# A recurrent attention block and a mixture of experts on one core: turning x later in six units, a small transfer's user later in one, a warm-up in shorter matmuls

## The chip, the core and the metric

The kernel runs on one core of one Trainium2 chip. The core has a matrix engine (PE, with its weight loads PEld), a vector engine (DVE), a scalar engine (ACT), a programmable engine (POOL) and SP, which here only issues transfers. Each engine works through its own list of instructions in order; semaphores tie them together. The metric is the device time of one execution in microseconds, inputs and outputs in the chip's memory, as the median of repeated runs.

## What is computed

```python
# q, k, v, f_logit: (4, 8, 768, 48);  f = sigmoid(f_logit)
for t in range(S):
    state = f[:, :, t, :, None] * state + einsum('bhd,bhe->bhde', k_t, v_t)
    y[:, :, t] = einsum('bhd,bhde->bhe', q_t, state)
x = y.transpose(0, 2, 1, 3).reshape(3072, 384)
g   = argmax(x @ w_group)                 # 4 groups
e   = argmax(x @ w_expert[g])             # 4 experts in the group
out = g_weight * e_weight * (relu(x @ w1[g, e]) @ w2[g, e])    # 384 -> 1024 -> 384
```

All numbers are 32-bit. g_weight and e_weight are the softmax values of the chosen group and expert.

## The kernel before

The kernel has two halves. The first turns the recurrence into matmuls over chunks of 128 time steps and routes the tokens as it goes; the second runs the experts.

**Units.** The sequence has 6 chunks (NC) and 4 batch entries, taken two at a time: 12 units (NU), unit i being chunk i // 2 and half i % 2. For each unit there is a set of stages, written as Python generators. Each token in an order string, such as `t` or `x-1`, runs one further piece of one stage: the letter names the stage, the number is added to the unit of the turn (`x-1` in turn 5 works on unit 4). The stages that matter here:

- `l` (L584): SP issues the loads of k, q, v and of the next f.
- `c` (L593), `g` (L600): clamp f on DVE; then on ACT Exp and Ln, on PE the running sum `cs` (L616), on ACT the two exponentials eq and kh (L617, L618) of each of two batch entries; the last row of eq is sent to the small tile `ends` (L623), from POOL for units below 10 and from ACT for units 10 and 11 (`side`, L573).
- `m` (L630): q and k times these factors, on DVE.
- `t` (L642): four groups of turnings tr_q, tr_k on PE and their copies to Tq and Tk on ACT.
- `b` (L654): in odd units, `ends` is turned on PE (gt, L659) and copied on ACT to `decays` (L660).
- `z` (L663): two ACT copies that shift half of v.
- `s` (L670): scores ap on PE, masked on DVE to am (L692 in units 3 to 8, L707 in the others).
- `n` (L710): first piece, 32 matmuls ds on PE; second piece, state = (state + ds) * decays on DVE (L727, L728).
- `w` (L733): first piece, y from the state (L742); second piece, y from am and v (L754 or L746), copied on ACT to xT (L757).
- `d` (L760): logits lT from xT (L770), ACT copy lgT (L772); then lg (L775) and a DVE sum (L776). After an odd unit this starts the routing of the chunk.
- `x` (L782): *turning of outputs to rows*. Eight turnings x_ps on PE in two groups (L795), three ACT copies to rows in on-chip memory (L797, L800), and as a third piece, from unit 8 (KEPT) on, a transfer of the rows to x_dram (L803). Rows of units 0 to 7 are kept and sent by SP in turns 8 and 9 (`o`, L810).
- `r`: the next piece of routing (`route`, L188): A and B, maxima and one-hot choices on DVE; C, the ranks rk in five bf16 matmuls (L213, L215) and an Exp on ACT (L216); D, the places (pick, keys, run, L221 to L224) on DVE, and in turn 9 also the choice of the first experts (`rank_early`, `named`: who, L300); E and F, tables on DVE; G, the weight of each token (L246 to L254) and its transfer; H, a table tb on PE.
- `1` to `4` (`load_next`, L817): weights of the first two experts, by `who`.

**What sets the order.** Under `manual_schedule` the four engines PE, DVE, ACT and SP run their instructions in the order in which the Python code issues them, so an order string is the order on all four queues at once. POOL's order and the waits come from the framework. Turns 3 to 12 use EVEN, ODD or an entry of ORDERS (L847 to L855). BEGIN (L843) covers units 0 to 2.

**Buffers.** All outputs of PE but one share 7 banks (tag "bank", L81); a new tile takes a bank whose tile is done with.

**The second half.** 16 experts are sorted by load; one takes pass after pass of up to 230 tokens through two layers (hp L450, yo L486 or L471), gathered by POOL from x_dram and scattered by POOL to the output.

**Warm-up.** Before the first data are there, PE runs ten matmuls of ones into one bank (L891 to L893).

Of the kernel before, what the change touches and what calls it, by code (L numbers as in the profile page):

```python
# [18 lines left out]
P = 128  # L19
# [4 lines left out]
def kernel(  # L24
# [12 lines left out]
    nc = tc.nc  # L37
# [39 lines left out]
    def const(shape, dtype, name):  # L77
        return cp.tile(shape, dtype, tag=name, name=name)

    def bank(shape, name):  # L80
        return ps.tile(shape, FP32, tag="bank", name=name)  # L81
# [11 lines left out]
    onesb = const([P, P], BF16, "onesb")  # L93
# [305 lines left out]
    def fetch(pool, rows, n, top=N, late=False):  # L399

        w = {"n": n, "pool": pool, "early": top < N, "late": late, "blocks": [(j, min(P, n - j * P)) for j in range((n + P - 1) // P)]}
        w["x"] = pool.tile([P, len(w["blocks"]), RW], FP32, tag="xg", bufs=2 if pool is ep else 6, name="xg")
        for j, m in w["blocks"]:
            nc.gpsimd.indirect_dma_start(out=w["x"][:, j, :], out_offset=None, in_=x_dram[0:1 + top, :], in_offset=bass.IndirectOffsetOnAxis(ap=rows[:, j:j + 1], axis=0))  # L404
        return w
# [124 lines left out]
    with ExitStack() as fast:  # L530
# [31 lines left out]
        NU = len(units)  # L562
# [21 lines left out]
        def load(i, names):  # L584
            c, s = units[i]
            w = live.setdefault(i, {"v": pads["v"][i % 4], "qh": pads["qh"][i % 3]})
            for nm in names:
                if nm not in w:
                    w[nm] = sb.tile([P, 2, H, D], FP32, tag="ld_" + nm, bufs=3 if nm == "f" else 2, name="ld_" + nm)
                for b in parts(i) if nm == "f" else (slice(0, 2),):  # L590
                    nc.sync.dma_start(out=heads(w[nm][:, b])[:, :, 0:D], in_=SRC[nm][2 * s + b.start:2 * s + b.stop, :, c * P:(c + 1) * P, :].rearrange("b h t d -> t (b h) d"))
# [241 lines left out]
        def advance(gens):  # L833
# [10 lines left out]
            t1 t1 t1 t1 b1 c2 g2 g2 s1 s1 s1 s1 p d0 g2 g2 n0 n1 w1 w1 m2 m2 l4 n1  # L844
            d0 x1 x1 t2 t2 t2 t2 c3 g3 g3 x1 s2 s2 s2 s2 w2 g3 g3 d1 w2 n2 m3 m3 c4 g4 g4""".split()
        BEGUN = 3
        EVEN = "l+2 d-2 n-1 r r r x-1 x-1 t t t t g+1 g+1 x-1 r z s s w s s c+2 d-1 g+2 w g+2 n m+1 m+1".split()  # L847
        ODD = "l+2 d-2 r r x-1 x-1 t t t t b n-1 g+1 g+1 x-1 r z s s w s s c+2 d-1 g+2 w g+2 n m+1 m+1 r n".split()
        ORDERS = {
            NU - 4: "l+2 o d-2 n-1 r r r x-1 x-1 t t t t g+1 g+1 x-1 r z s s w s s c+2 d-1 g+2 w g+2 n m+1 m+1".split(),  # L850
            NU - 3: "l+2 o d-2 r r x-1 x-1 t t t t b n-1 r g+1 g+1 x-1 r s s s s c+2 w d-1 g+2 w g+2 n m+1 m+1 r n".split(),
            NU - 2: "d-2 r x-1 x-1 r t t t t g+1 g+1 r 1 x-1 s s s s w d-1 w n m+1 m+1 2 3".split(),
            NU - 1: "d-2 r r n-1 x-1 x-1 t t t t r x-1 r s s s s 4 w b d-1 w r r".split(),
            NU: "d-2 r e d-1 x-1 x-1 d-1 x-1 r r r e e r e r r e r r e r e r r e e e e e".split(),
# [3 lines left out]
        def step(nm, i):  # L858
            if nm == "r":
                advance(routes)  # L860
            elif nm == "e":
                next(first[0], None)
            elif nm == "p":
                next(pad)
            elif nm == "o":
                send_kept(i - (NU - 4))
            elif nm in "1234":
                load_next(*((0, 1), (1, 1), (0, 2), (1, 2))[int(nm) - 1])
            elif nm == "h":
                next(turning)  # L870
            elif 0 <= i < NU:
                if nm == "l":

                    load(i, ("k", "qh"))
                    if i + 1 < NU:
                        load(i + 1, ("f",))
                    load(i, ("v",))
                    return
                if (nm, i) not in steps_of:
                    steps_of[nm, i] = STAGES[nm](i)  # L880
                next(steps_of[nm, i], None)
# [6 lines left out]
        load(1, ("qh", "k"))  # L888
        load(2, ("f",))
        load(1, ("v",))  # L890
        warm = bank([P, 4, P], "warm")  # L891
        for _ in range(10):
            nc.tensor.matmul(warm, lhsT=onesb, rhs=onesb.unsqueeze(1).broadcast_to((P, 4, P)), start=True, stop=True)  # L893
        for tok in BEGIN:
            step(tok[0], int(tok[1:] or 0))
        for i in range(BEGUN, NU + 1):
            if i == BEGUN:
                nc.sync.dma_start(out=x_dram[0:1, 0:DM].rearrange("o (h d) -> o h d", d=D), in_=blank[:, 0:D].unsqueeze(1).broadcast_to((1, H, D)))
                nc.sync.dma_start(out=x_dram[0:1, DM:RW], in_=blank[:, D:D + 2])
            for tok in ORDERS.get(i, ODD if i % 2 else EVEN):  # L900
                step(tok[0], i + int(tok[1:] or 0))
# [62 lines left out]
    for n in range(GE - 1):  # L964
        w = ws[n]
# [105 lines left out]
    with tc.If(more > 0), ExitStack() as late:  # L1071
# [5 lines left out]
        with tc.For_i(0, last, 1) as i:  # L1077
# [14 lines left out]
            w = fetch(ep, row, P, late=True)  # L1092
# [32 lines left out]
```

## Time and profile before

| what | value |
|---|---|
| median of 3 runs | 418.54 us (418.44 to 419.1) |
| the profiled execution: its time | 417.84 us |
| the profiled execution: span, first to last instruction | 416.0 us |
| mean granted PE clock | 0.994 |
| PE busy / DVE busy / ACT busy, 40 to 60 us | 19.45 / 15.31 / 16.38 of 20 us |
| the same, 100 to 120 us | 18.98 / 17.23 / 12.26 of 20 us |
| the same, 160 to 180 us | 17.41 / 10.61 / 3.16 of 20 us |
| first half ends (last lg of the logits) | about 132 us |
| x_ps: turnings, median ns of one | 96, 273 (starts 109 ns apart) |
| ACT copies of x: 384 wide / 192 wide | 478 / 332 to 339 ns |
| longest DVE wait for `decays` (4 in all) | 6.0 us in total, 1.72 in unit 9 |
| warm-up: 10 matmuls, ns min/median/max | 379 / 631 / 631, first at 1.05, last at 4.7 us |

How to read it: the span is shorter than the time because the time holds what lies around the instructions. A matmul's duration includes its way through the array; neighbours overlap, so the distance between two starts tells the pace. "Busy" of PE counts overlapping ends as one. A line in order of time has the start, the duration (or the union of several), the engine, the line of the kernel, the operation with output and inputs, and, in brackets, how long the engine had been idle before it and what ended that. "ACTq" or "SPq" is the engine's sequencer, at work on something like the issue of a transfer.

### The profile page before, as it was taken

The numbers are of one execution on the slowest core, as the hardware profiler recorded it, in microseconds if no ns is written. First come the engines' busy times: TensorE is split into PE (matmuls) and PEld (weight loads), VectorE is DVE, ScalarE is ACT, GpSimd is POOL, SyncE is SP. The second block draws the span as 40 slices with busy tenths as digits, with TensorE's granted clock in tenths as the row PEclk, the third lists the DMA queues.
The fourth block names the chain that finished last, engine by engine and source line by source line (L and its number), as shares of the span: only waits on it lengthen the run. The fifth ranks groups of instructions, "written<-read, shape, count | busy, mean of one in ns | idle before, by whom it ended". The sixth has DMA issues, their size and how long they took to land.

```text
span 416.0 us, 10268 instructions
## 1 busy us (share of the span) xinstructions
PE 404.0 (97%) x4143; PEld 371.9 (89%) x4143; DVE 264.3 (64%) x783; ACT 162.2 (39%) x365; POOL 85.7 (21%) x132
## 2 busy tenths in 40 slices
PE   8999999999999997999999999999999999999994
PEld 3888888888888966989999999999999999999992
DVE  6666878787998702440799767485595595584230
ACT  6777878887664211211223122222231232232220
POOL 5000010101040174001041221311321230120230
PEclk9999999999999999999999999999999999999999
DMA  9999987879869499855729467586495596485010
GB/s 191 208 216 197 201 179 147 164 159 289 244 225 378 163 337 345 318 179 184 271 84 335 137 245 265 164 315 208 170 348 169 217 352 200 173 318 162 28 48 24
DMA packets 132146, 88.99 MB, mean 214 GB/s; under 512 B 102582, under 2 KB 122748, under 8 KB 132090
## 3 DMA queue, kind: packets, MB, share of 16 engines
q1 hardware_dynamic: 125666, 75.50, 60.6%
q0 software_dynamic: 5792, 11.92, 9.5%
q10 hardware_dynamic: 632, 0.83, 0.6%
q8 instruction: 35, 0.57, 0.6%
q14 instruction: 21, 0.17, 0.1%
HBM read 78.71 MB, written 9.83 MB: 213 GB/s over the span
## 4 chain that ended last, share of the span: by engine, by line
PE 48%; issue 30%; DMA 9%; POOL 6%; DVE 3%; POOLq 1%; another core or an unknown queue 1%; ACT 1%; SPq 0%; ACTq 0%; DVEq 0%
PE hp L450 12%; PE yo L486 6%; DMA out_dram<-yt,xg 6%; PE yo L471 4%; PE cs L616 4%; POOL out_dram L461 4%; PE ap L704 3%; PE y L746 3%; POOL xg L404 2%; PE x_ps L795 2%; PE tr_q L650 2%; PE tr_k L650 2%; PE y L742 2%; PE ap L689 2%; PE y L754 2%
## 5 line engine op out<-in xcount | busy, mean ns | idle before, releaser
L450 PE MATMUL hp<-xe,w 128*128 128x128 f32 (+14 forms) x864 | 141.3, 323 | 2.6 <-issue 1.8
L450 PEld LDWEIGHTS hp<-xe,w 128*128 128x128 f32 x864 | 137.4, 192 | 4.5 <-issue 2.4
L486 PE MATMUL yo<-h,w 128*128 128x230 f32 (+13 forms) x672 | 115.8, 333 | 0.0
L433 DVE STREAM_TRANSPOSE yr<-yT 32x192 f32<-32x192 f32 (+1 forms) x208 | 70.5, 339 | 70.5 <-ACT yT L487 67.9
L486 PEld LDWEIGHTS yo<-h,w 128*128 128x128 f32 x672 | 113.7, 190 | 0.2
L451 ACT ACTIVATE h<-hp 128x256 f32<-128x256 f32 (+14 forms) x72 | 34.2, 478 | 109.1 <-PE hp L450 100.2
L426 DVE STREAM_TRANSPOSE xe<-xg 32x192 f32<-32x192 f32 (+1 forms) x208 | 69.6, 335 | 8.7 <-PE hp L450 5.8
L461 POOL DMA_INDIRECT out_dram<-yt,xg x32 | 34.5, 1078 | 156.1 <-ACT yt L458 150.5
L487 ACT COPY yT<-yo 128x230 f32<-128x230 f32 (+13 forms) x42 | 13.5, 325 | 80.5 <-PE yo L486 80.5
L404 POOL DMA_INDIRECT xg<-x_dram,rows_p x30 | 29.6, 986 | 51.1 <-DMA out_dram<-yt,xg 25.7
L471 PE MATMUL yo<-w,h 128*128 128x384 f32 x64 | 21.3, 486 | 0.0
L707 DVE TENSOR_TENSOR am<-ap,tri 128x512 f32<-128x512 f32 x24 | 15.1, 688 | 7.3 <-PE ap L704 7.3
L616 PE MATMUL cs<-ld_f,tri 128*128 128x384 f32 x48 | 18.5, 505 | 0.5 <-POOL blank L177 0.3
L471 PEld LDWEIGHTS yo<-w,h 128*128 128x128 f32 x64 | 11.9, 190 | 7.4
L458 ACT ACTIVATE yt<-yr,xg 128x384 f32<-128x384 f32 (+13 forms) x26 | 14.4, 604 | 5.4 <-DVE yr L433 5.4
L623 POOL DMA_DIRECT2D ends<-eq x10 | 5.4, 542 | 52.2 <-ACT eq L617 52.2
L692 DVE TENSOR_TENSOR am<-ap,seen 128x384 f32<-128x384 f32 x24 | 12.2, 551 | 5.5 <-PE ap L689 5.5
L757 ACT COPY xT<-y 128x512 f32<-128x512 f32 x24 | 13.4, 587 | 5.0 <-PE y L746 4.4
L651 ACT COPY Tk<-tr_k 128x512 f32<-128x512 f32 x24 | 15.2, 636 | 0.0
L651 ACT COPY Tq<-tr_q 128x512 f32<-128x512 f32 x24 | 15.0, 625 | 0.4 <-PE tr_q L650 0.3
L441 DVE COPY xe<-xg_ps 128x384 f32<-128x384 f32 (+1 forms) x4 | 2.1, 535 | 20.5 <-remote 9.7
L650 PE MATMUL tr_q<-ident,qh 128*128 128x128 f32 x96 | 14.5, 274 | 0.5 <-issue 0.5
(187 smaller groups left out, 448.4 us busy)
## 6 DMA issues: line engine op xcount, KB each, us to landing
w<-in_moe_w_dram SPq DMA_DIRECT2D x34, 1536.0 KB, 7.2
qh<-in_q_dram SPq DMA_DIRECT2D x12, 384.0 KB, 6.1
ld_k<-in_k_dram SPq DMA_DIRECT2D x12, 384.0 KB, 4.4
v<-in_v_dram SPq DMA_DIRECT2D x12, 384.0 KB, 5.4
ld_f<-in_f_logit_dram SPq DMA_DIRECT2D x11, 384.0 KB, 5.5
x_dram<-x_kept SPq DMA_DIRECT2D x2, 1536.0 KB
x_dram<-x POOLq DMA_DIRECT2D x2, 384.0 KB
x_dram<-x ACTq DMA_DIRECT2D x2, 384.0 KB, 7.4
```

The source lines that it names most:

```text
L404: nc.gpsimd.indirect_dma_start(out=w["x"][:, j, :], out_offset=None, in_=x_dram[0:1 + top, :], in_offset=bass.IndirectOffsetOnAxis(ap=rows ...
L426: squares(w, lambda n, k_, rk, g, rg: nc.vector.transpose(out=xT[rg, 0:n, k_], in_=x[rk, 0:n, g]))
L433: squares(w, lambda n, k_, rk, g, rg: nc.vector.transpose(out=y[rk, 0:n, g], in_=yT[rg, 0:n, k_]))
L450: nc.tensor.matmul(hp[:, o, :], lhsT=w1[:, ko, (f + o) * P:(f + o + 1) * P], rhs=w["xT"][:, ko, :], start=(ko == 0), stop=(ko == KO - 1))
L451: nc.scalar.activation(h[:, f:f + 2, :], hp, AF.Relu)
L461: sent = nc.gpsimd.indirect_dma_start(out=out, out_offset=bass.IndirectOffsetOnAxis(ap=w["x"][0:m, j, DM + 1:RW].bitcast(U32), axis=0), in ...
L471: nc.tensor.matmul(yp, lhsT=w["h"][:, fo, :], rhs=w2[:, fo, :], start=(fo == 0), stop=(fo == FO - 1))
L486: nc.tensor.matmul(yp, lhsT=w2[:, fo, m * P:(m + 1) * P], rhs=w["h"][:, fo, :], start=(fo == 0), stop=(fo == FO - 1))
L616: nc.tensor.matmul(cs.rearrange("t h d -> t (h d)"), lhsT=tri, rhs=nl[:, b], start=True, stop=True)
L650: nc.tensor.transpose(out=pt[:, a, :], in_=w[nm + "h"][:, b, 2 * a:2 * a + 2, :].rearrange("t r d -> t (r d)"), identity=ident)
L651: nc.scalar.copy(w["T" + nm][:, b], pt)
L707: nc.vector.tensor_tensor(am[:, r], ap[r], tri.unsqueeze(1).broadcast_to((P, HP, P)), OP.mult)
```

## The change

Three things are edited. In turns 3 to 8 the three pieces of `x-1` go from ahead of (two) and behind (one) `t` and `g+1` to behind the masked scores and `d-1`, ahead of `w`'s second piece; `d-1` goes ahead of `c+2`; in ODD one `r` (piece C of the routing) goes behind `x-1` too. In turn 9, `b n-1` goes from ahead of `r g+1 g+1` to behind it. The warm-up becomes 40 matmuls of 128 columns in place of 10 of 512.

```diff
-        EVEN = "l+2 d-2 n-1 r r r x-1 x-1 t t t t g+1 g+1 x-1 r z s s w s s c+2 d-1 g+2 w g+2 n m+1 m+1".split()
-        ODD = "l+2 d-2 r r x-1 x-1 t t t t b n-1 g+1 g+1 x-1 r z s s w s s c+2 d-1 g+2 w g+2 n m+1 m+1 r n".split()
+        EVEN = "l+2 d-2 n-1 r r r t t t t g+1 g+1 r z s s w s s d-1 x-1 x-1 x-1 c+2 g+2 w g+2 n m+1 m+1".split()
+        ODD = "l+2 d-2 r r t t t t b n-1 g+1 g+1 z s s w s s d-1 x-1 x-1 x-1 r c+2 g+2 w g+2 n m+1 m+1 r n".split()
         ORDERS = {
-            NU - 4: "l+2 o d-2 n-1 r r r x-1 x-1 t t t t g+1 g+1 x-1 r z s s w s s c+2 d-1 g+2 w g+2 n m+1 m+1".split(),
-            NU - 3: "l+2 o d-2 r r x-1 x-1 t t t t b n-1 r g+1 g+1 x-1 r s s s s c+2 w d-1 g+2 w g+2 n m+1 m+1 r n".split(),
+            NU - 4: "l+2 o d-2 n-1 r r r t t t t g+1 g+1 r z s s w s s d-1 x-1 x-1 x-1 c+2 g+2 w g+2 n m+1 m+1".split(),
+            NU - 3: "l+2 o d-2 r r x-1 x-1 t t t t r g+1 g+1 b n-1 x-1 r s s s s c+2 w d-1 g+2 w g+2 n m+1 m+1 r n".split(),
...
-        warm = bank([P, 4, P], "warm")
-        for _ in range(10):
-            nc.tensor.matmul(warm, lhsT=onesb, rhs=onesb.unsqueeze(1).broadcast_to((P, 4, P)), start=True, stop=True)
+        warm = bank([P, P], "warm")
+        for _ in range(40):
+            nc.tensor.matmul(warm, lhsT=onesb, rhs=onesb, start=True, stop=True)
```

## The prediction, made before the changed kernel was run

> **What bounds the kernel now.** I read the page first, then a table of stretches, then the tensor engine, the scalar engine and the vector engine in order of time around unit 9, where the one visible hole lies. The page's first line says that the whole kernel is the tensor engine's:
>
> ```profile
> PE 404.0 (97%) x4143; PEld 371.9 (89%) x4143; DVE 264.3 (64%) x783; ACT 162.2 (39%) x365; POOL 85.7 (21%) x132
> ```
>
> By stretches (PE busy, then weight loads, DVE, ACT, POOL, granted clock, DMA share, GB/s), units 3 to 8 run from about 37 to 99 us:
>
> ```profile
> 40.00:60.00 20.00, 19.45 (x478) 16.65 (x477) 15.31 (x43) 16.38 (x38) 2.04 (x4) 1.00 0.91 182
> 60.00:80.00 20.00, 19.99 (x484) 17.26 (x482) 15.87 (x45) 16.53 (x38) 2.01 (x4) 1.00 0.76 153
> 80.00:100.00 20.00, 19.99 (x484) 17.26 (x483) 15.87 (x45) 16.52 (x38) 2.01 (x4) 1.00 0.97 218
> 100.00:120.00 20.00, 18.98 (x304) 16.00 (x304) 17.23 (x54) 12.26 (x31) 2.44 (x4) 1.00 0.78 207
> ```
>
> PE has no hole worth a name in the six units whose order changes: 0.53 us with no releaser at 56.5 (in unit 4), nothing after. A busy PE need not be a PE at its pace, so I also looked at starts: eight turnings x_ps start every 109 ns, in every unit; y L754 takes 1.64 us from first to last start in units 3, 5, 6, 7 and 8 alike, although DVE reaches its masks at different times in even and odd units. So PE is paced by its own work there. The 1.0 us missing from the last row is in unit 9. PE in order of time (start, us, what, idle before it and what ended it):
>
> ```profile
> 101.41 0.60 PE L650 MATMUL tr_k<-ident,kh 128*128 128x128 f32 x4
> 103.03 0.20 PE L659 MATMUL gt<-ident,ends 16*128 16x16 f32 x1 [1.02 <-DMA ends<-eq]
> ...
> 103.31 0.57 PE L616 MATMUL cs<-ld_f,tri 128*128 128x384 f32 x1
> ```
>
> PE stands before gt until the small transfer of `ends` lands (the chain of waits has it issued at 95.89 and on its way 7.01 us). Last to next start is 1.30 us. What follows on ACT, then on DVE:
>
> ```profile
> 102.23 0.67 ACT L651 COPY Tk<-tr_k 128x512 f32<-128x512 f32 x1
> 103.27 0.17 ACT L660 COPY decays<-gt 128x16 f32<-128x16 f32 x1 [0.38 <-PE gt L659]
> 103.34 0.27 ACT L216 ACTIVATE dl<-dl 128x80 f32<-128x80 f32 x1
> 104.24 0.49 ACT L617 ACTIVATE eq<-cs 128x384 f32<-128x384 f32 x1 [0.63 <-PE cs L616]
> 104.63 0.48 ACT L618 ACTIVATE kh<-cs 128x384 f32<-128x384 f32 x1
> 105.00 0.50 ACT L617 ACTIVATE eq<-cs 128x384 f32<-128x384 f32 x1
> 105.37 0.51 ACT L618 ACTIVATE kh<-cs 128x384 f32<-128x384 f32 x1
> 105.53 0.76 ACTq L623 DMA_DIRECT2D ends<-eq  x1
> ```
>
> ```profile
> 101.21 0.55 DVE L727 TENSOR_TENSOR st<-st,ds 128x384 f32<-128x384 f32 x1
> 103.47 0.56 DVE L728 TENSOR_TENSOR st<-st,decays 128x384 f32<-128x384 f32 x1 [1.72 <-ACT decays L660]
> 103.95 0.22 DVE L221 TENSOR_TENSOR pick<-rk,run 128x64 f32<-128x64 f32 x1
> ...
> 106.78 0.16 DVE L300 CAST who<-names 1x2 int32<-1x2 f32 x1
> 106.85 2.46 DVE L707 TENSOR_TENSOR am<-ap,tri 128x512 f32<-128x512 f32 x4
> ```
>
> From 103.47 to 109.3 DVE has no idle time. Its four masks am begin the moment `who` is done, and PE takes them at once (lT, then y L746, which needs am):
>
> ```profile
> 107.80 0.64 PE L770 MATMUL lT<-xT,gw 128*32 128x128 f32 x16
> 108.37 0.44 PE L746 MATMUL y<-am,v 128*64 128x128 f32 x4
> ```
>
> The first two am end near 108.07, the fourth at 109.31; y's second half starts near 109.4. So in unit 9 PE and DVE are level to 0.3 us and then to 0.1 us: whatever moves L728 moves PE.
>
> **What the Trainium skill says.** (1) Perfetto Trace Analysis, Sequencer Loop: a sequencer reads in order; an engine instruction is pushed into the engine's queue, a control instruction is executed by the sequencer before it reads on. The trace agrees for DMA issues: SP's start at 68.86, 69.32 and 70.56, each when the one before it (0.37, 1.15 us) is over. A copy behind L623 on ACT should thus wait out its 0.76 us. (2) TensorE: Matmul & The Clock Gate, "Why this matters for your kernels": PE should have no idle gaps over about 3 us, or its clock falls to half. The trace agrees: PE was mostly idle from 159.6 to 164.3, and the granted clock is 0.50 in 166 to 168. (3) The same page, Back-to-back issue gap: cold, matmuls start N/1.2 ns apart. The ten warm-up matmuls (N = 512) started some 0.43 us apart: agrees.
>
> **The change, part by part.**
>
> *x-1 in units 3 to 8.* The same eight turnings and three ACT copies, later. Removed: lg to x_ps 0.16 us, 0.87 us of x_ps, 0.11 to tr_q; lT to y 0.20. Added: lg to tr_q 0.16, lT to x_ps 0.20 (so at 130.9), x_ps to y 0.1 to 0.2. Sum per unit 0 to +0.09, six units 0 to +0.5. I take 0. Cover for what loses its distance: tr_q would start where x_ps did, 68.88 in unit 6; qh was ready at 67.96, kh at 68.83 against tr_k at 69.32, and both come some 0.87 us sooner, since the second ap, and behind it am, ld_f, qh and kh, come sooner in the unit. ACT's copies of x (1.1 us) fall into its waits before lgT (0.89) and before L607 (0.66); then L607 ends at about the time y is done, so xT is not late. If that cover is gone, xT is late by tenths. Banks: between y and its copy five others must serve am, lT, x and rk; the two of the second ap are free when the masks are done, before rk. SP: x_kept of unit 7 is ready near 97, and SP sends it at 106.13: covered. POOL's `ends` and meta come up to 0.87 us sooner in unit 8.
>
> *The r moved in units 3, 5, 7.* Five matmuls of rk (0.12 us) and one Exp (0.3 us), no DVE work; its user, pick, comes after kh. Nothing.
>
> *b and n-1 in unit 9.* Gain on PE: behind tr_k now come rk (0.12) and cs (1.4), so `ends` has landed when gt comes near 103.4. 1.30 less 0.1 of handover: 1.2 us. Loss: decays, a copy on ACT, now stands behind dl, eq, kh, eq, kh *and* the issue of unit 10's `ends`. Step by step: tr_k ends near 101.85, rk, cs from 102.0; the old eq began 0.93 after cs, so eq at 102.97 (ACT is also busy till then: Tk at 102.23 takes a slot of 0.48, dl 0.26); kh 103.36, eq 103.73, kh 104.10. The issue waits for eq (0.53 after its start, as before): 104.26 to 105.02. decays 105.05 to 105.3. L728 at 105.3 instead of 103.47: **+1.8 us**. Behind it on DVE, in order: pick to `who` (2.9 us), am, ld_f, qh, kh. PE could have y L746 at 107.2, but the first two am end near 109.87 and the fourth at 111.1: y's second half starts at 111.2, not 109.4. So PE saves 1.2 us, waits 2.7, and leaves unit 9 1.8 us late. Lower bound of this term: if the issue holds up nothing, decays runs at 104.5 and L728 at 104.8, +1.3.
>
> *After that.* Units 10 to 12 are dense on PE (holes of 0.26 and less), so nothing is won back; `who_late` for the early weights, who at 143.71 and all loads behind them hang on the same DVE chain and shift with it, as does the stretch 158 to 164, whose releaser the trace can't name. +1.8 goes to the end.
>
> *Warm-up.* 40 x 128 columns instead of 10 x 512: the same 5,120. Own weight loads: 40 instead of 10, 147 ns each, beside matmuls. Before, it ended at 5.06 and cs began at 5.35. If loads are hidden (107 ns a matmul by that same page): the same end. If not (254 ns until the clock rises at 4.5): end near 8, 1.6 us lost on the chain that runs through cs at 6.42. From below: 0, since cs waits for its data. I take 0. Sixty more PE instructions also shift where PE's instructions are fetched; the 0.53 us in unit 4 may go or come twice: -0.5 to +0.5.
>
> *Sum.* Against the profiled execution (span 416.0, time 417.84): span 417.8, time 419.6. The three runs have the median 418.54, so 418.54 + 1.8 = **420.3**.
>
> **Rivals.**
> - *Clock falls too.* PE's 2.7 us of idle in unit 9 is near the gap of point 2. Half speed for 3.4 us costs up to 1.7 us: 421.9. For it: a stretch in which PE worked about a third of the time did it at 164. Against: that one lasted 4.7 us.
> - *The other side: the hole before gt is all that counts, 417.2.* It needs L728 not to be late: decays would have to run by 103.5, which nothing on ACT's list allows unless L728's follower on DVE isn't what y waits for. PE's 1.2 us would then reach the end. It decides once am's start is set by ap (near 105.7) and not by `who`. A vanished 0.53 us in unit 4 would add to it. I also count here a shorter stall at 158 to 164.
> - *Given back: 418.6.* The delay is 1.3, and 0.5 in unit 4 and some of the later stall offset it.
>
> **How the numbers follow.** Forecast 0.45, clock 0.22, given back 0.10, faster 0.23. The forecast's own range is 419.5 to 421.1 (+1.3 from below, +0.5 of turnings and +0.3 of fetch from above). For 8 in 10 the clock case comes in whole and about half of the faster one: 417.4 to 422.2. A measurement of this kernel tells about 0.2%, 0.84 us, from no change: slower by more 0.65, within 0.12, faster by more 0.23.
>
> **What would show it.** In unit 9: no DMA wait before gt; DVE idle of about 3.5 us before L728, ended by ACT's decays, which starts right after the ACT issue of `ends`; PE idle of 2 to 3 us before y L746, ended by DVE. Units 3 to 8: 10.0 to 10.3 us each, as before, x_ps between lT and y, no new wait above 0.1 us. Wrong if decays starts before 104, if y L746 follows lT at once, or if PE is idle before tr_q, tr_k or rk in units 3 to 8.

## The result, and the profile after

| | before | after |
|---|---|---|
| median | 418.48 us (417.19 to 419.45, 9 runs) | 420.55 us (419.35 to 421.89, 9 runs) |
| the profiled execution: time / span | 417.84 / 416.0 | 421.04 / 419.2 |
| mean granted clock in it | 0.994 | 0.989 |

The changed kernel takes 1.0048 times as long, with an interval of 1.0029 to 1.0068: 2.0 us more, between 1.2 and 2.8. The two profiled executions stand 3.2 apart, since that of before is 0.64 below its median and that of after 0.49 above.

The page of the changed kernel, its line of busy times and its line of the granted clock in tenths over 40 slices:

```profile
PE 406.1 (97%) x4173; PEld 375.7 (90%) x4173; DVE 264.8 (63%) x783; ACT 162.8 (39%) x365; POOL 85.3 (20%) x132
PEclk9999999999899999899999999999999999999998
```

The busy times hardly differ. The clock line shows two dips, in the eleventh slice (105 to 115 us) and in the seventeenth; the second belongs to the stall near 160 us that the kernel before has too, the first is new.

**Where the time went.** I followed one landmark per unit, the first matmul ds (L722), through both traces. Before, those of units 2 and 8 start at 36.77 and 98.20, that of unit 9 at 110.30; after, at 37.18, 98.67 and 113.09. So the changed kernel is 0.41 late ahead of turn 3 already, loses 0.06 over the six units with the turning moved, and 2.32 in unit 9 (2.54 up to the next lg, since its ds start while the last of y is still running). Then nothing comes back: lg of units 10 and 11 is 2.97 late both times, the span 3.2.

Unit 9 of after, first ACT and then DVE (start, duration, what, idle before it and what ended that):

```profile
103.17 0.35 ACT L216 ACTIVATE dl<-dl 128x80 f32<-128x80 f32 x1
103.38 0.53 ACT L617 ACTIVATE eq<-cs 128x384 f32<-128x384 f32 x1
...
104.51 0.55 ACT L618 ACTIVATE kh<-cs 128x384 f32<-128x384 f32 x1
104.70 0.76 ACTq L623 DMA_DIRECT2D ends<-eq  x1
105.50 0.17 ACT L660 COPY decays<-gt 128x16 f32<-128x16 f32 x1 [0.45 <-ACT kh L618]
```

```profile
101.68 0.55 DVE L727 TENSOR_TENSOR st<-st,ds 128x384 f32<-128x384 f32 x1
105.71 0.56 DVE L728 TENSOR_TENSOR st<-st,decays 128x384 f32<-128x384 f32 x1 [3.48 <-ACT decays L660]
106.19 0.22 DVE L221 TENSOR_TENSOR pick<-rk,run 128x64 f32<-128x64 f32 x1
...
109.00 0.16 DVE L300 CAST who<-names 1x2 int32<-1x2 f32 x1
109.08 2.46 DVE L707 TENSOR_TENSOR am<-ap,tri 128x512 f32<-128x512 f32 x4
```

The copy of decays now stands behind six things on ACT (dl, two pairs of eq and kh, and an issue), and its bracket hides the last of them: what it waited for by the profile is kh, over at 105.06, but between the two stands the issue of a transfer, 104.70 to 105.46. L728 waits 3.48 for it (1.72 before). Everything that follows on DVE, down to `who` and the masks am, is as dense as before and starts later. PE, which has nothing to wait for at gt any more:

```profile
103.92 0.23 PE L659 MATMUL gt<-ident,ends 16*128 16x16 f32 x1
104.08 2.06 PE L704 MATMUL ap<-Tq,Tk 48*128 48x128 f32 x32
106.06 1.10 PE L742 MATMUL y<-Tq,st 48*64 48x128 f32 x32
107.09 0.65 PE L770 MATMUL lT<-xT,gw 128*32 128x128 f32 x16
109.81 3.55 PE L746 MATMUL y<-am,v 128*64 128x128 f32 x31 [2.07 <-DVE am L707]
```

The hole ahead of gt is gone, and a hole of 2.07 ahead of y L746 is there instead. And the matmuls of y then take 3.55. The same matmuls take 1.97 where the masks are ready (e4 below) and 2.9 where the masks come as late as here but the clock is full (e6 below); here they run at half the clock. In windows of 3.41 us (PE busy, weight loads, DVE, ACT, POOL, granted clock, DMA share, GB/s):

```profile
102.46:105.88 3.42, 3.42 (x43) 2.58 (x39) 0.17 (x1) 2.77 (x8) 0.00 (x0) 1.00 1.05 246
105.88:109.29 3.41, 1.86 (x54) 1.30 (x50) 3.07 (x14) 0.27 (x1) 0.00 (x0) 1.00 0.83 188
109.29:112.71 3.42, 2.90 (x24) 2.60 (x26) 3.42 (x6) 0.66 (x1) 0.00 (x0) 0.50 1.03 371
```

After a window in which PE was busy 1.86 of 3.41 comes one at 0.50.

### The profile page after: what moved, and what is told of

It reads as the page before. It is cut to its first block, busy times and chain, and to the rows that moved or that the text cites. A ratio compares the mean times of both kernels' runs of the same rounds, so it can differ in the third digit from the quotient of the medians.

```text
span 419.2 us, 10334 instructions
## 1 busy us (share of the span) xinstructions
PE 406.1 (97%) x4173; PEld 375.7 (90%) x4173; DVE 264.8 (63%) x783; ACT 162.8 (39%) x365; POOL 85.3 (20%) x132
## 3 DMA queue, kind: packets, MB, share of 16 engines
HBM read 78.71 MB, written 9.83 MB: 211 GB/s over the span
## 4 chain that ended last, share of the span: by engine, by line
PE 50%; issue 29%; DMA 7%; POOL 6%; DVE 4%; POOLq 1%; another core or an unknown queue 1%; ACT 1%; ACTq 0%
PE hp L450 12%; DMA out_dram<-yt,xg 7%; PE yo L486 6%; PE yo L471 4%; POOL out_dram L461 4%; PE cs L616 3%; PE y L746 3%; PE x_ps L795 3%; PE y L754 2%; PE ap L704 2%; PE ap L689 2%; POOL xg L404 2%; PE ds L722 2%; PE y L742 2%; PE tr_k L650 2%
## 5 line engine op out<-in xcount | busy, mean ns | idle before, releaser
L746 PE MATMUL y<-am,v 128*64 128x128 f32 x192 | 13.5, 293 | 2.1 <-DVE am L707 2.1
L746 PEld LDWEIGHTS y<-am,v 128*64 128x64 f32 x192 | 11.7, 148 | 3.8 <-DVE am L707 3.2
```

The lines of the kernel that those rows point to most:

```text
L746: nc.tensor.matmul(ys[b][DP * h:DP * h + DP, a, :], lhsT=w["v"][:, b, 2 * a + (b ^ h), :], rhs=w["am"][b][:, b ^ h, a, :], start=(c == 0 a ...
```

## The experiments

They ran on three other chips, four kernels on each, beside the kernel before. There the kernel before takes 412.43 (e1 to e4), 412.19 (e5 to e8) and 411.96 (e9 to e12); the stall near 160 and its half clock are absent in the traces of these runs. Ratios are to the kernel before on the same chip. My theory was that turn 9 makes the loss, by ACT's order (decays behind an issue) and DVE's order (all that PE needs behind L728); the rivals were the turning in six units, the warm-up, and the clock.

**e1: the turning alone** (turns 3 to 8 as in the change, the rest as before; of the three order strings edited, EVEN is shown).

```diff
-        EVEN = "l+2 d-2 n-1 r r r x-1 x-1 t t t t g+1 g+1 x-1 r z s s w s s c+2 d-1 g+2 w ...
+        EVEN = "l+2 d-2 n-1 r r r t t t t g+1 g+1 r z s s w s s d-1 x-1 x-1 x-1 c+2 g+2 w ...
```

> The kernel before with the turning moved in turns 3 to 8 alone. Theory (the loss sits in unit 9): 418.5 plus 0 to 0.3: in the changed kernel the even units 6 and 8 took 10.29 us from ds to ds instead of 10.05, with PE waiting for val before tb; three such waits cost 0.7, the 0.6 us stall of unit 4 may or may not be there, and the ends transfer, issued up to 0.5 us sooner, takes as much off the wait before gt. Rival (the move of the turning is what costs): at least +1.5, 420 or more.

Measured: 412.47 (14 runs), ratio 1.0006, 0.9996 to 1.0016. No change that can be told. But the trace has a longer wait, three times, in the even units. Waits from 36 to 99 us (in total, times, longest), first of e5, which is the kernel before, then of e1:

```profile
PEld L261 <- DVE val L243: 1.9, 3, 0.6
```

```profile
PEld L261 <- DVE val L243: 2.6, 3, 0.9
PE tb L261 <- DVE val L243: 0.8, 3, 0.3
```

tb, the matmuls of piece H, now comes 0.87 earlier after `t`, and `val` on DVE doesn't. The weight loads waited before too, at no cost, since PE was still busy; what is new is that PE itself waits. In starts of PE it costs 0.22 to 0.24 in each of units 4, 6 and 8 (10.29 from ds to ds, where an undisturbed even unit of the old order takes 10.07). What pays for it is e5's matter.

**e2: turn 9 alone.**

```diff
-            NU - 3: "l+2 o d-2 r r x-1 x-1 t t t t b n-1 r g+1 g+1 x-1 r s s s s c+2 w d-1 g+2 w g+2 n m+1 m+1 r n".split(),
+            NU - 3: "l+2 o d-2 r r x-1 x-1 t t t t r g+1 g+1 b n-1 x-1 r s s s s c+2 w d-1 g+2 w g+2 n m+1 m+1 r n".split(),
```

> The kernel before with b and n-1 of turn 9 moved alone. Theory: L728 starts 1.8 us later in the unit than before, ended by ACT's decays behind the issue of ends; ds of unit 9 1.8 us later if PE's clock holds, 2.5 if it falls in the gap before y L746: median 420.2 to 421. Rival (the move of the turning costs, unit 9 gains the hole of 1.2): 417.3.

Measured: 415.37 (6 runs), ratio 1.0072, 1.0048 to 1.0096: +2.9, the whole of the loss. In its trace the stretch from the lg in turn 9 to the lg in turn 10 takes 13.82, as in the changed kernel on these chips (13.81 in e6). Its runs part by the clock: 413.94 and 414.61 at a mean clock of 1.000; 415.61 to 416.2 at 0.992 and 0.993; one between them, 415.12 at 0.996.

**e3: the warm-up alone.**

```diff
-        warm = bank([P, 4, P], "warm")
-        for _ in range(10):
-            nc.tensor.matmul(warm, lhsT=onesb, rhs=onesb.unsqueeze(1).broadcast_to((P, 4, P)), start=True, stop=True)
+        warm = bank([P, P], "warm")
+        for _ in range(40):
+            nc.tensor.matmul(warm, lhsT=onesb, rhs=onesb, start=True, stop=True)
```

> The kernel before with the 40 short warm-up matmuls alone. Theory: the matmuls end at the same time, but the full clock comes one window later (6.9 instead of 4.5 us), so the first units start about 0.4 us late: 418.9. Rival: the moment of the clock's rise is a matter of chance in each execution, and the medians are equal, 418.5, whatever this profile shows.

Measured: 411.95 (14 runs), ratio 0.9992, 0.9981 to 1.0003. The 0.4 that the profiled pair shows in front isn't the warm-up's: here the clock is up at 3.96 and the 40 matmuls are over at 4.83, while the kernel before has it up at 4.48 in one trace and at 6.44 in another.

**e5, e6, e7: the kernel before, the changed kernel, and the changed kernel with unit 10's `ends` issued from POOL.** e7 takes the issue out of ACT's list and leaves the order:

```diff
-                    side(i).dma_start(out=ends[c][...], in_=eq[P - 1:P]...)
+                    side(i - 1).dma_start(out=ends[c][...], in_=eq[P - 1:P]...)
```

> The kernel before itself, for a trace of it on the chip of the runs beside it. Where the stretch at 157 to 164 us (PE waiting for nothing shown, then half clock) is absent, as in the four runs so far, about 412.4; where it is there, about 418.5.

> The changed kernel itself, beside the runs of one edit each. Theory: the sum of the parts, 2.0 to 2.9 over the kernel before, nearly all of it from unit 9, and the executions split by the granted clock: those at full clock some 1.5 below those that lost it in the gap before y L746. Rival: on a chip without the later stall the loss is gone or doubled, if that stall rather than unit 9 made it.

> The changed kernel with the transfer of ends of unit 10 issued by POOL instead of ACT. Theory (the issue's 0.76 us stands ahead of decays on ACT's sequencer): decays starts right behind kh, L728 0.6 to 0.65 us sooner, the gap before y L746 1.7 instead of 2.3, fewer executions at the lower clock: 0.6 to 1.5 below the changed kernel. Rival (the copy waits for kh's end or for gt, not for the issue): decays at the same distance from kh, and the time of the changed kernel.

Measured: 411.89 (one run) for the kernel before; 415.56 (6 runs), ratio 1.0079, 1.0062 to 1.0095, for the changed one, which is 3.3 more, above the 2.0 to 2.9 expected; 413.69 (7 runs), ratio 1.0039, 1.0025 to 1.0053, with the issue on POOL. ACT in e6, then in e7:

```profile
104.22 0.55 ACT L618 ACTIVATE kh<-cs 128x384 f32<-128x384 f32 x1
104.41 0.76 ACTq L623 DMA_DIRECT2D ends<-eq  x1
105.21 0.17 ACT L660 COPY decays<-gt 128x16 f32<-128x16 f32 x1 [0.45 <-ACT kh L618]
```

```profile
104.10 0.55 ACT L618 ACTIVATE kh<-cs 128x384 f32<-128x384 f32 x1
104.47 0.24 ACT L660 COPY decays<-gt 128x16 f32<-128x16 f32 x1
```

From the start of kh to the start of decays it is 0.99 with the issue between them and 0.37 without. From the lg in turn 9 to the lg in turn 10 (the texts on record call them lg of unit 9 and of unit 10) it is 13.81 in e6, 13.27 in e7 and 11.48 in e5: the issue is worth 0.54 of a loss of 2.33. The rest is put down to the place of decays and L728; e4 and e8 test that. The median falls by 1.9, more than 0.54; the hole ahead of y L746 is shorter (1.79 from lT's last matmul, not 2.34), and of e7's seven runs one stands at the lower clock (414.86 at 0.993), of e6's six three (415.8 to 416.1 at 0.992 and 0.993). The clock is not all of it: the runs at 0.996 and more also stand 1.1 apart (means 413.7 and 414.8), and half of that is not explained.

e5 shows two things more. gt waits for nothing there, nor in the other traces with the old turn 9 (e1, e3, e9):

```profile
101.60 0.60 PE L650 MATMUL tr_k<-ident,kh 128*128 128x128 f32 x4
102.13 0.23 PE L659 MATMUL gt<-ident,ends 16*128 16x16 f32 x1
```

The hole before it, 1.30 from start to start in the first trace of before, belongs to that chip or that execution. Without it there is nothing to be won, and unit 9 of the changed kernel costs 2.3, not 1.8. And units 3 to 8 of e5 (ds of unit 2 to ds of unit 8) take 60.87 without a pause, where those with the turning moved take 61.50 in e1, e6 and e7 alike: 3 x 0.22 more. But e5 has a pause of 0.62 directly after, inside ds of unit 8, and the five other traces of the old order (before, e2, e3, e4, e8) take 61.20 to 61.61: PE loses 0.1 to 0.6 in a unit or two, mostly among the matmuls y L754 and with no releaser, never in the same place. With e5's pause counted, the mean of the six is 61.4. The five traces with the turning as in the change (after, e1, e6, e7, e12) lose nothing in that way and take 61.48 to 61.50, which fits e1's ratio of 1.

**e4, e8: decays late, but with nothing of PE's behind it.** If DVE's order is the cause, the state's steps can go behind the masks, at no wait for y. e4 moves `b` behind `g+1` and `n-1` behind `s`; e8 lets `c+2` go ahead, `b` behind `g+1` and `n-1` to the end:

```diff
-            NU - 3: "l+2 o d-2 r r x-1 x-1 t t t t b n-1 r g+1 g+1 x-1 r s s s s c+2 w d-1 g+2 w g+2 n m+1 m+1 r n".split(),
+            NU - 3: "l+2 o d-2 r r x-1 x-1 t t t t r g+1 g+1 b x-1 r s s s s n-1 c+2 w d-1 g+2 w g+2 n m+1 m+1 r n".split(),
...
+            NU - 3: "l+2 o d-2 r r c+2 x-1 x-1 t t t t r g+1 g+1 b x-1 r s s s s w d-1 g+2 w g+2 n-1 n m+1 m+1 r n".split(),
```

> The kernel before with b of turn 9 behind the running sums, as in the change, but the state's two DVE operations behind the scores, so that neither the places nor the masks stand behind decays. Theory: PE keeps the 1.2 us of the hole before gt and y L746 follows lT with no wait: 417.2 to 417.5, faster than both kernels. Rival (PE's time in unit 9 is bound by something else, such as ap or the banks, so that taking the wait away gives nothing): 418.5.

> The kernel before with b of turn 9 behind the running sums, the state's two DVE operations behind the masks of unit 9, and the clamp of f of unit 11 in DVE's idle time ahead of the places. Theory: in the run with the state behind the scores 0.55 us were given back because xT stood behind an Exp that waited for the clamp; with the clamp early, x_ps follows lg at once, and ds to ds of unit 9 is 0.6 to 0.7 us shorter than in the kernel before: 411.7 against 412.4. Rival (what is won in unit 9 is lost in unit 10, where PE then waits for qh and kh): the same as before within 0.2.

Measured: e4 412.37 (14 runs), ratio 0.9996, 0.9985 to 1.0008; e8 411.87 (14 runs), ratio 0.9996, 0.9983 to 1.0008. In e4, y follows lT at once and ds of unit 9 ends early, but the next group gives it back:

```profile
107.18 1.97 PE L746 MATMUL y<-am,v 128*64 128x128 f32 x32
108.98 0.89 PE L722 MATMUL ds<-v,kh 128*48 128x48 f32 x32
109.80 0.33 PE L775 MATMUL lg<-ident,lgT 128*128 128x128 f32 x1
110.52 1.14 PE L795 MATMUL x_ps<-ident,xT 128*128 128x128 f32 x8 [0.39 <-ACT xT L757]
```

x_ps waits for xT. ACT copies xT behind the Exp L607, and that waits for DVE's clamp of f (`c+2`), which now stands behind the masks and both steps of the state:

```profile
109.14 0.85 ACT L607 ACTIVATE ld_f<-ld_f 128x768 f32<-128x768 f32 x1 [1.56 <-DVE ld_f L597]
```

From lg to lg turn 9 takes 10.76 instead of e5's 11.48, but the next turn 10.47 instead of 9.83. With `c+2` in front (e8) x_ps comes 0.17 after lg; turn 9 again takes 10.76, and the next one 0.17 more than in e5, so that 0.55 should be left. On the medians neither kernel can be told from the one before: e8's interval reaches from 0.7 below to 0.3 above.

**e9, e10, e11: the late tb, both orders together, and that with the new warm-up.** The turning is moved as in the change, and in the even turns tb goes behind `w`, where `val` is ready; e10 adds turn 9 of e8, e11 the warm-up of e3. EVEN of the changed kernel, then of these:

```diff
-        EVEN = "... t t t t g+1 g+1 r z s s w s s d-1 x-1 x-1 x-1 c+2 g+2 w g+2 n m+1 m+1".split()
+        EVEN = "... t t t t g+1 g+1 z s s w r s s d-1 x-1 x-1 x-1 c+2 g+2 w g+2 n m+1 m+1".split()
```

> The turning moved behind d-1 in turns 3 to 8 as in the change, but the step of piece H's second half (tb) goes from ahead of the table z to behind its w in the even turns. Theory: the matmuls of tb no longer wait for val (0.22 to 0.24 in each even unit of the run with the turning moved alone), units of 10.07 and 10.23 alternate without the stray pauses of the old order, so ds of unit 2 to ds of unit 8 take 60.9 where the turning moved alone took 61.5; the time is 0.4 to 0.6 below the kernel before. Rival: val, or the table behind it, is late in the new place too, or the pauses come back: within 0.2 of the kernel before.

> The even and odd turns of the run beside it, and turn 9 in the order that lets the state's steps go last (c+2 ahead of x-1, b behind g+1, n-1 behind the second g+2). Theory: the two gains stand in different units and add: 0.5 from units 3 to 8 and 0.7 from unit 9 (lg of unit 9 to lg of unit 10 in 10.76, not 11.48): 1.0 to 1.3 below the kernel before, about 0.3 per cent. Rival: what is won comes back as a pause further on, or the single gains are not there on the median: within 0.2 of the kernel before.

> The same with the 40 matmuls of 128 columns in front in place of 10 of 512. Theory: the width of the matmuls in front decides nothing; the clock rises at some time between 4 and 7 whichever stands there: equal to the run without it within 0.3. Rival: with the wide form the clock rises earlier: 0.4 longer than the run without it.

Measured: e9 411.99 (13 runs), ratio 0.9999, 0.9990 to 1.0007; e10 411.09 (13 runs), ratio 0.9976, 0.9967 to 0.9986; e11 411.10 (13 runs), ratio 0.9980, 0.9971 to 0.9988. In e9 the wait for `val` is gone; what the weight loads of tb still wait for:

```profile
PEld L261 <- DVE meta L254: 0.5, 3, 0.2
```

Units 3 to 8 take 61.13 (61.02 in e10 and e11), not the 60.9 expected: the even units take 10.13 instead of 10.07. The wait for `meta` stands there; that it makes the difference is not shown. In e9 one odd unit also has a pause of 0.1. The 61.13 is 0.3 less than the mean of the old order, and the median doesn't show it (its interval: 0.4 below to 0.3 above); e9 went as its rival had it. e10 is 0.9 below the kernel before (0.6 to 1.4) and as much below e9. Its theory had 1.0 to 1.3; the traces make it 0.55 from unit 9 (10.76 instead of 11.48, 0.17 given back) and 0.4 from units 3 to 8 (61.02 against 61.4). How the 0.9 splits is not settled, since e8 and e9 alone are within no change. e11 stands on e10, as the theory had it. Unit 9 of e10, DVE and then PE:

```profile
104.59 0.16 DVE L300 CAST who<-names 1x2 int32<-1x2 f32 x1
104.66 2.46 DVE L707 TENSOR_TENSOR am<-ap,tri 128x512 f32<-128x512 f32 x4
107.06 0.53 DVE L727 TENSOR_TENSOR st<-st,ds 128x384 f32<-128x384 f32 x1
107.69 0.56 DVE L728 TENSOR_TENSOR st<-st,decays 128x384 f32<-128x384 f32 x1
```

```profile
106.22 0.64 PE L770 MATMUL lT<-xT,gw 128*32 128x128 f32 x16
106.79 1.97 PE L746 MATMUL y<-am,v 128*64 128x128 f32 x32
108.59 0.89 PE L722 MATMUL ds<-v,kh 128*48 128x48 f32 x32
```

decays comes as late as in the changed kernel (behind the issue, at 104.63, 1.59 after gt), and nobody minds: the masks are done before y wants them, and L728 waits for nothing. This is the best of the kernels tried, on this chip.

**e12: the hole filled.** 32 matmuls of ones, whose output nobody reads, between the logits and y L746 of the changed kernel.

```diff
-... s s s s c+2 w d-1 g+2 w g+2 ...
+... s s s s c+2 w d-1 k g+2 w g+2 ...
+            elif nm == "k":
+                fill = bank([P, P], "fill")
+                for _ in range(32):
+                    nc.tensor.matmul(fill, lhsT=onesb, rhs=onesb, start=True, stop=True)
```

> The changed kernel with 32 matmuls of the 128x128 ones, into a bank that nobody reads, between the logits of unit 10 and y L746, where TensorE stands still for 2.0 to 2.3 (work is added, none is left out). 40 of them took 4.4 at the half clock in front, so 32 take about 1.8 at the full one and fit into the hole. Theory: the hole is what makes the clock fall in about half of the changed kernel's executions (time 415.8 to 416.1 at a mean clock of 0.992 to 0.993, 414.4 to 414.7 above 0.995): with the hole filled no execution stands below 0.995, and the median is 414.4 to 414.8, about 0.8 below the changed kernel's 415.56 against the kernel before. Rival: the clock falls by itself, or for the load: executions at 0.993 are as many as before and the median is 415.4 or more.

Measured: 415.97 (6 runs), ratio 1.0092, 1.0075 to 1.0109; three runs at 0.994 to 0.995 (416.6 to 416.8), three at 0.997 to 0.998 (415.1 to 415.3). The experiment missed its object:

```profile
109.40 2.82 PE L872 MATMUL fill<-onesb 128*128 128x128 bf16 x32 [2.07 <-DVE am L707]
112.15 2.69 PE L746 MATMUL y<-am,v 128*64 128x128 f32 x32
```

The new tile took one of the seven banks, and that bank came free with the masks. So the hole stayed, the fill came after it, and neither theory was put to the test. That filling the hole would hold the clock is not shown. Its trace is still of use, together with those of e6 and e7. Stretches of 3.41 us that end where the clock can change (see the last section), first e6's two around the hole, then e7's second one, then e12's:

```profile
105.37:108.78 3.41, 2.08 (x58) 1.52 (x54) 3.02 (x13) 0.28 (x2) 0.00 (x0) 1.00 0.97 195
108.78:112.19 3.41, 2.40 (x32) 1.92 (x34) 3.41 (x7) 0.43 (x1) 0.00 (x0) 1.00 0.97 347
```

```profile
107.77:111.18 3.41, 2.06 (x26) 1.58 (x28) 3.34 (x9) 0.09 (x1) 0.00 (x0) 1.00 0.89 318
```

```profile
106.84:110.25 3.41, 1.34 (x32) 1.17 (x26) 3.20 (x10) 0.27 (x1) 0.00 (x0) 1.00 0.99 287
110.25:113.67 3.42, 3.42 (x34) 3.22 (x33) 3.35 (x8) 0.84 (x1) 0.00 (x0) 0.50 0.73 261
```

In e6 the same hole lies across a window's edge: 2.08 and 2.40 busy, and the clock stays at full. In e12 it lies inside one window, 1.34 busy, and the next is at half although PE works all through it.

## Why the prediction was right, and where it was not

- **Turn 9, +1.8 by L728: right.** From ds of unit 8 to L728 it is 5.27 before and 7.04 after, +1.77. decays at 105.50, directly behind the issue, was foreseen at 105.05 (the front was 0.4 late); the lower bound, decays at 104.5 if the issue held nothing up, is what e7 made of it (104.47). PE's wait of 2.7 became 2.3.
- **"+1.8 goes to the end": right.** Units 10 and 11 shift by 2.97 each, as unit 9 did.
- **PE saves 1.2 at gt: right in the profiled pair only.** On the other chips there is no such hole, and e6's unit 9 loses 2.33. The prediction took one execution's transfer for the kernel's property.
- **The issue holds ACT up: right.** From before, only SP's issues, each behind the one ahead of it, spoke for it; that a copy on ACT waits too is what e6 against e7 shows (0.99 against 0.37).
- **The turning in six units, nothing: right on the sum (e1, 1.0006), wrong on the way.** I wrote that no new wait above 0.1 would come; the even units lose 0.22 to 0.24 to `val`. I had looked for what the *moved* pieces need and not for what now comes earlier because they left: tb. The pauses without a releaser, which I put at -0.5 to +0.5, are missing in exchange (61.50 against a mean of 61.4).
- **Warm-up, nothing: right** (e3; e11 against e10 0.0). The 0.41 in front of the profiled pair goes with the moment when the clock came up, 6.89 against 4.48; it is not shown to be all of it, since e11, with the earliest rise (3.86), has its ds of unit 2 at 36.98 and e10, at 5.18, at 36.78.
- **The clock holds: wrong in the profiled execution.** I had given its fall 0.22: a hole of 2.7 was near the 3 us of the page "TensorE: Matmul & The Clock Gate", and the earlier fall had 4.7 us of idling. The step that failed is that a gap's length decides, and the trace of before already spoke against it: from 159.6 to 164.3 PE worked 2.1 of the 4.7 us (more than the "about a third" I wrote), and its longest single gap was 1.14. That was no agreement with a rule on gaps over 3 us. The fall cost some 0.6 to 0.8 directly (y L746 to ds 3.28 in after, 2.71 in e6; to lg 4.31 and 3.53). The means of the runs at 0.992 and 0.993 stand 1.1 above those of the others in e6, 1.3 in e2. That those runs lost the clock in unit 9 is inferred from the mean clock; the profiled executions of e2 and e6 kept it there.
- **So the total, 420.3 against 420.55, is in part luck.** The +1.8 was meant for executions that keep the clock. As far as the mean clock tells these apart: of the nine runs of the changed kernel, the five at a mean clock of 0.992 to 0.994 average 419.9, 1.4 above the median before, and the four at 0.989 and 0.990 average 421.3, 2.8 above. The median lies between the two groups, and the interval of 1.2 to 2.8 can't tell 1.8 from 1.8 with a part of a falling clock. The lower end of the forecast's range, 419.5, does not follow from the terms given for it: +1.3 gives 419.8.

## What to carry to other kernels

When a step is moved later on an in-order engine, list what is queued behind it there, transfer issues among what it moves past, and ask for whom that queue works: here decays itself could be 1.7 late at no cost, once the masks stood ahead of the instruction that waits for it (e10). When a step is moved away, look at its old followers: they come earlier, and their inputs may not. And a hole of 2 us on TensorE is priced with the chance that it also halves the clock after it.

## What the runs showed of the hardware that was not expected

- **The clock changes at the edges of windows, and no idle window is needed for it to fall.** In all 14 traces the stretches between two changes of the clock are multiples of 3.413 us: 30, 1, 16, 1 and 72 windows in after, 47, 1 and 72 in before, 31, 1 and 88 in e12, 118 or 119 in the eleven others. The Trainium skill ("TensorE: Matmul & The Clock Gate", Part 1) has this window, free-running, of 3413 ns; the traces agree. It calls for an idle window before the clock falls; here a window with PE busy for 1.86 (after), 1.34 (e12) or 1.56 of 3.41 (before, 161.50 to 164.91) was enough, while windows around the hole of unit 9 with 2.06 or more (e2, e6, e7) kept it. The measurement decides. Since the windows' phase differs by execution (the clock first comes up anywhere from 3.86 to 6.89), a hole of 2.3 drops the clock in some executions and not in others.
- **The busy share alone is not the rule.** Near the end of e2, PE is busy for 1.51 of a window, less than in after, and the clock stays full in the next window; the same with 1.66 in e7 (404.73 to 408.14). The window of e2 and the next:

```profile
405.67:409.09 3.42, 1.51 (x5) 0.57 (x3) 0.00 (x0) 0.58 (x1) 0.96 (x1) 1.00 0.02 7
409.09:412.50 3.41, 0.00 (x0) 0.00 (x0) 0.00 (x0) 0.00 (x0) 0.03 (x1) 1.00 0.12 45
```

Only after the second of these, which is wholly idle, does the clock fall. The matmuls are others there (128x384; in after's window 48x128 and 128x128); whether that or something else counts, no run here shows.
- **An issue on ACT holds the next ACT instruction up for 0.62** (e6 against e7), close to the 0.76 that it lasts.
- **The first chip is 1.5% slower.** The kernel before takes 418.48 there and 411.96 to 412.43 on three others. On the first, PE stands still for 2.6 of the 4.7 us from 159.6 to 164.3 (in the changed kernel the same stretch comes 3 us later), and the half clock follows; why, no run here shows.
- **Pauses of PE of 0.1 to 0.6 without a releaser** come and go from one trace to the next; the five traces with the turning as in the change have none in units 3 to 8. What they are stays open.
